# Decode attention on one core: tiles of two adjacent heads with 16 KB runs, softmax groups of four tiles, query broadcast on TensorE, MLP weights overlaid on value buffers

## The chip, the cores and the metric

The kernel runs on one core of one Trainium2 chip. The metric is the device time in microseconds (us) of that core; the median of several executions is quoted, with the lowest and the highest beside it. All executions that are compared were in the chip's fast state, and each kernel was timed beside the kernel before on the same chip. Where two changed kernels from different calls are compared, they ran on different chips; the median of the kernel before stayed between 1364.6 and 1365.5 us on all of them.

The engines are called by their names in the profile: PE is TensorE (matmuls), DVE is VectorE, ACT is ScalarE, POOL is GpSimd, SP is SyncE, which here only issues the DMA transfers. SPq is the queue in which SP's transfers stand.

## The reference

One decoding step for a batch of 8: attention with a cache of 4096 positions and 32 heads of 128, plus an MLP on the same normalized input. Everything is bf16.

```python
def reference(A_x, A_k_cache, A_v_cache, A_wq, A_wo, B_x, B_w1, B_b1, B_w2, B_b2):
    # x (8,1,640); k_cache, v_cache (8,32,4096,128); wq (640,4096); wo (4096,640)
    # w1 (640,1728); w2 (1728,640)
    xn = layernorm(A_x)
    y = layernorm(xn)
    h = gelu(y @ B_w1 + B_b1)
    q = (xn @ A_wq) as (8, 32, 1, 128)
    p = softmax(q . k_cache * 128 ** -0.5)
    o = p . v_cache
    return A_x + (o as (8, 1, 4096)) @ A_wo + (h @ B_w2 + B_b2)
```

The two caches are 268 MB each (8 x 32 x 4096 x 128 x 2 bytes). Each byte of them is used once. The kernel is a stream of 537 MB through the DMA engines, with a little arithmetic beside it.

## The kernel before

A head, here, is one (head, batch element) pair: 256 of them, each with 1 MB of K and 1 MB of V. Two heads are loaded by one transfer, and they are the same head of two neighbouring batch elements, so they are not adjacent in memory. The rearrangement gives each of the 128 partitions 32 consecutive positions of 128 bf16, a run of 8 KB, for each of the two heads.

```python
NK = 6; NV = 6                       # buffers of one head: three pairs of K, three of V

def pair_src(cache, n):
    g, i = n // B, n % B
    return cache[i:i + 2, g].rearrange("n (p j) d -> p n j d", p=P)    # two runs of 8 KB for a partition

def sp_v(n):                                                           # sp_k(n) is alike
    def fn(e):
        s = n % NV
        if n >= NV:
            e.wait(pv_done, tk[("pv", n + 1 - NV)])                    # PV must have freed the buffers
        t = ld_v[s // 2].sig(e.dma_start(V_sb[:, s:s + 2, :, :], pair_src(A_v_cache, n)))
        ...
```

The scores of a head are split over two engines. PE transposes 8 of the 32 blocks of K and multiplies them with the query (not shown). DVE does the other 24: it multiplies K with the query, which stands in all partitions, halves the product by an addition, and reduces it.

```python
def dve_qk(n):
    ...
    tm = km_done.sig(e.tensor_tensor(Y_sb[:, :, :], K_sb[:, n % NK, JP:NJ, :],
             qbc_sb[:, g % 2, i * P:(i + 1) * P][:, None, :].to_broadcast([P, ND, P]), ALU.mult))
    ...
    ty = d_sem.sig(e.tensor_tensor(Y2_sb[...], Y_sb[:, :, 0:P // 2], Y_sb[:, :, P // 2:P], ALU.add))
    ...
    kd_done.sig(e.tensor_reduce(Sd_sb[:, g % 3, i, :], Y2_sb[:, n % 2, :, :], AX.X, ALU.add))
```

The query gets into all partitions in three steps: PE transposes it into one row, DVE copies the row out of PSUM, the memory into which PE writes (`dve_qn`), and POOL broadcasts it (`pool_qb`). A softmax group is eight heads: one maximum over all of them, then the exponentials on ACT. The sum over V (called PV) follows on PE, 8 matmuls for a head. ACT copies the result out as `E_sb`, and four small matmuls (`pe_ex`) put it back into columns.

Each engine's program is a list sorted by a position. PV runs 16 heads (`2 * GP`) behind the scores, and so do the V loads:

```python
UH = 3; GP = B * UH
add("sp", -10.0, sp_mlp)                                             # MLP weights, b1 element by element
for n in range(0, NH, 2):
    add("sp", (-300.0 + n) if n == 0 else UH * (n - NK) + UH + 1.0, sp_k(n))
    add("sp", UH * (n - NV) + 2 * GP + UH + 2.5, sp_v(n))
...
for g in range(G):
    cb = float(g * GP + GP)
    ...
    for i in range(B):
        p0 = cb + GP + UH * i + (UH - 1)
        add("pe", p0, pe_PV(g * B + i))
        add("act", p0 + 0.6, act_pv(g * B + i))
        add("pe", p0 + 2.5, pe_ex(g * B + i))
```

Of the kernel before, what the change touches and what calls it, by code (L numbers as in the profile page):

```python
# [6 lines left out]

BF = mybir.dt.bfloat16
F32 = mybir.dt.float32
I32 = mybir.dt.int32  # L10
# [3 lines left out]
P = 128  # L14
# [3 lines left out]
class _Sem:  # L18

    def __init__(self, es, nc, name, step=1):  # L20
        self.h = es.enter_context(nc.semaphore(name))
        self.n = 0
        self.step = step

    def sig(self, inst):
        inst.then_inc(self.h, self.step)
        self.n += self.step
        return self.n


class _RecInst:
    def __init__(self, call):
        self.call = call

    def then_inc(self, sem, n):
        self.call[3].append((sem, n))
        return self


_OPS = ("wait_ge", "dma_start", "matmul", "transpose", "tensor_copy", "tensor_scalar",  # L40
        "tensor_tensor", "tensor_reduce", "tensor_tensor_reduce", "scalar_tensor_tensor",
        "reciprocal", "memset", "activation", "iota", "partition_broadcast")


class _Rec:

    def __init__(self):
        self.calls = []
        self.waited = {}
        (self.wait_ge, self.dma_start, self.matmul, self.transpose, self.tensor_copy,  # L50
         self.tensor_scalar, self.tensor_tensor, self.tensor_reduce, self.tensor_tensor_reduce,
         self.scalar_tensor_tensor, self.reciprocal, self.memset, self.activation,
         self.iota, self.partition_broadcast) = (self._mk(n) for n in _OPS)

    def wait(self, sem, ticket):
        if ticket > self.waited.get(sem.h, 0):
            self.waited[sem.h] = ticket
            self.wait_ge(sem.h, ticket)

    def _mk(self, name):  # L60
        def f(*a, **k):
            call = (name, a, k, [])
            self.calls.append(call)
            return _RecInst(call)
        return f


def _replay(e, calls):
    for name, a, k, incs in calls:
        if name == "wait_ge":  # L70
            e.wait_ge(*a, **k)
            continue
        if name == "dma_start":
            inst = e.dma_start(*a, **k)
        elif name == "matmul":
            inst = e.matmul(*a, **k)  # L76
        elif name == "transpose":
            inst = e.transpose(*a, **k)  # L78
        elif name == "tensor_copy":
            inst = e.tensor_copy(*a, **k)  # L80
        elif name == "tensor_scalar":
            inst = e.tensor_scalar(*a, **k)
        elif name == "tensor_tensor":
            inst = e.tensor_tensor(*a, **k)  # L84
        elif name == "tensor_reduce":
            inst = e.tensor_reduce(*a, **k)  # L86
        elif name == "tensor_tensor_reduce":
            inst = e.tensor_tensor_reduce(*a, **k)
        elif name == "scalar_tensor_tensor":
            inst = e.scalar_tensor_tensor(*a, **k)  # L90
        elif name == "reciprocal":
            inst = e.reciprocal(*a, **k)  # L92
        elif name == "memset":
            inst = e.memset(*a, **k)
        elif name == "activation":
            inst = e.activation(*a, **k)  # L96
        elif name == "iota":
            inst = e.iota(*a, **k)
        elif name == "partition_broadcast":
            inst = e.partition_broadcast(*a, **k)  # L100
        else:
            raise ValueError(name)
        for sem, n in incs:
            inst.then_inc(sem, n)


def bass_parallel_sum__gqa_block_cached__mixer_channel_mlp__decode_kernel(
# [16 lines left out]
    assert DH == P and SK % P == 0 and D % P == 0 and B <= 8  # L124
    NJ = SK // P
    TPB = 8
    BANKS = ((0, 8),)
    EVE = (1,)
    UH = 3
    BPH = len(BANKS)  # L130
    JP = sum(b[1] for b in BANKS)
    ND = NJ - JP
    assert NJ == 32 and B * JP <= 512
# [3 lines left out]
    G = H  # L137
    NH = G * B
    NBANK = NH * BPH
    GB = B * BPH  # L140
    SCALE = float(DH) ** -0.5

    NK = 6
    NV = 6
    NS = 4
    NTR = 2
    LAGT = 1
    HPP = 4 if H % 4 == 0 else 1
    NPIECE = H // HPP
    NWO = 4  # L150
    VLAG = 2 * B
# [4 lines left out]
    with ExitStack() as es:  # L156
# [3 lines left out]

        K_sb = sb("K_sb", [P, NK, NJ, P], BF)
        V_sb = sb("V_sb", [P, NV, NJ, P], BF)
        KT_sb = sb("KT_sb", [P, NS, TPB, P], BF)
        wq_sb = sb("wq_sb", [P, 2, DC, HPP * P], BF)
        wo_sb = sb("wo_sb", [P, NWO, D], BF)
        w1_sb = sb("w1_sb", [P, DC, F], BF)
        w2_sb = sb("w2_sb", [P, FC, D], BF)
        b1T_bf = sb("b1T_bf", [P, FC], BF)
        b1T_sb = sb("b1T_sb", [P, FC], F32)
# [3 lines left out]
        x32_sb = sb("x32_sb", [B, D], F32)  # L173
        sq_sb = sb("sq_sb", [B, D], F32)
        st_sb = sb("st_sb", [B, 8], F32)
        xn_bf = sb("xn_bf", [B, D], BF)
        y_bf = sb("y_bf", [B, D], BF)
        xnT_sb = sb("xnT_sb", [P, 2, DC, B], BF)
        qT_sb = sb("qT_sb", [P, H, B], BF)
        hT_sb = sb("hT_sb", [P, FC, B], BF)  # L180
        iota_i = sb("iota_i", [P, P], I32)
        iota_f = sb("iota_f", [P, P], F32)
# [3 lines left out]
        ones_f = sb("ones_f", [P, P], F32)  # L186
        zeros_bf = sb("zeros_bf", [P, P], BF)
        M1_sb = sb("M1_sb", [P, B], F32)
        M2_sb = sb("M2_sb", [B, 1], F32)
        D_sb = sb("D_sb", [B, B], F32)  # L190
        NB_sb = sb("NB_sb", [P, 3, B], F32)
        P_sb = sb("P_sb", [P, 3, B, NJ], BF)
        rs_sb = sb("rs_sb", [P, 3, 2, B], F32)
        Y_sb = sb("Y_sb", [P, ND, P], BF)
        Y2_sb = sb("Y2_sb", [P, 2, ND, P // 2], BF)
        Sd_sb = sb("Sd_sb", [P, 3, B, ND], F32)
        M1a_sb = sb("M1a_sb", [P, B], F32)
        M1b_sb = sb("M1b_sb", [P, B], F32)
        q_row = sb("q_row", [1, B * P], BF)
        qbc_sb = sb("qbc_sb", [P, 2, B * P], BF)  # L200
        rsum_sb = sb("rsum_sb", [P, B], F32)
        E_sb = sb("E_sb", [4, 2, 4 * P], BF)
        rinv_sb = sb("rinv_sb", [P, B], F32)
        oTn_sb = sb("oTn_sb", [P, 2, B], BF)
        resT_sb = sb("resT_sb", [P, DC * B], F32)
        out_sb = sb("out_sb", [B, D], BF)

        TR_ps = ps("TR_ps", [P, NTR, TPB * P], BF)
        S_ps = ps("S_ps", [P, 2, 512], F32)
        PV4_ps = ps("PV4_ps", [P, 2, 512], F32)  # L210
        CH_ps = ps("CH_ps", [P, 512], F32)
        ACC_ps = ps("ACC_ps", [P, 512], F32)
        TRF = TR_ps[:, :, :].bitcast(F32)
        M1T_ps = CH_ps[0:B, 0:P]
        NB_ps = CH_ps[:, 128:128 + B]
        RS_ps = CH_ps[:, 136:136 + 2 * B]
        QT_ps = CH_ps[:, 152:152 + HPP * B]
        HT_ps = CH_ps[:, 184:184 + FC * B]
        OT_c = CH_ps[:, 448:448 + B]
        QR_ps = CH_ps[:, 184:184 + B * P // 4].bitcast(BF)  # L220
        XT_ps = TR_ps[:, NTR - 1, 0:2 * DC * B]

        S = lambda name, step=1: _Sem(es, nc, name, step)
        assert B % 2 == 0 and NK % 2 == 0 and NV % 2 == 0 and NWO % 2 == 0 and G % 2 == 0
        ld_k = [S(f"ld_k{i}", 16) for i in range(NK // 2)]
        ld_v = [S(f"ld_v{i}", 16) for i in range(NV // 2)]
        ld_wq = [S(f"ld_wq{i}", 16) for i in range(2)]
        ld_wo = [S(f"ld_wo{i}", 16) for i in range(NWO // 2)]
        ld_x = S("ld_x", 16)
        pb_done = S("pb_done")  # L230
        e4_done = S("e4_done")
        ex_done = S("ex_done")
        km_done = S("km_done")
        kd_done = S("kd_done")
        qn_done = S("qn_done")
        ld_b1 = S("ld_b1", 16)
        ld_w1 = S("ld_w1", 16)
        ld_w2 = S("ld_w2", 16)
        out_done = S("out_done", 16)
        tr_done = [S("tr_done_d"), S("tr_done_a")]  # L240
        ev_done = [S("ev_done_d"), S("ev_done_a")]
        qk_done = S("qk_done")
        pv_done = S("pv_done")
        exp_done = S("exp_done")
        q_done = S("q_done")
        qe_done = S("qe_done")
        wo_done = S("wo_done")
        c1, c2, c3, c4, c5, c6, c7 = (S(f"c{i}") for i in range(1, 8))
        g_sem = S("g_sem")
        d_sem = S("d_sem")  # L250
        a_sem = S("a_sem")
        p_sem = S("p_sem")
        m_sem = S("m_sem")
        f_sem = S("f_sem")

        ch_read = [None]

        ch_wr = [None]

        def ch_write(e):  # L260
            if ch_read[0] is not None:
                e.wait(ch_read[0][0], ch_read[0][1])

        def ch_wrote(sem, ticket):
            ch_wr[0] = (sem, ticket)
            return ticket

        def ch_rwait(e):
# [627 lines left out]
```

## Time and profile before

| quantity | before |
|---|---|
| time, median of three (lowest to highest) | 1364.83 us (1364.8 to 1365.06) |
| span of the profiled execution | 1363.2 us |
| bytes moved by DMA | 553.13 MB |
| DVE busy | 1214.1 us, 89% |
| PE busy | 904.7 us, 66% |
| packets of 8 KB, duration (median) | 313 ns |

First come lines of the page. They give the span, the busy time of each engine with its share and its number of instructions, the DMA rate in 40 equal slices of the span, and DVE's product of K and the query (count, busy us, mean ns).

```profile
span 1363.2 us, 20347 instructions
...
PE 904.7 (66%) x8060; PEld 457.0 (34%) x8060; DVE 1214.1 (89%) x1162; ACT 547.3 (40%) x1555; POOL 70.8 (5%) x37
...
GB/s 344 267 360 421 420 415 421 419 421 419 416 421 419 421 419 417 422 419 418 411 419 419 421 419 415 421 417 421 410 417 421 418 421 417 420 421 419 421 388 211
...
L84 DVE TENSOR_TENSOR Y_sb<-K_sb,qbc_sb 128x3072 bf16<-128x3072 bf16 x256 | 446.8, 1745 | 1.1 <-POOL qbc_sb L100 1.1
...
```

The row of GB/s is what to look at. Thirty-five of the forty slices lie between 410 and 422. The first three and the last two do not. The engines by stretch say the same with chosen borders. The columns are: the stretch, its length, the busy us of PE, PE's weight loads, DVE, ACT and POOL (instructions in brackets), the granted clock, the busy share of the DMA engines, and GB/s.

```profile
...
0.00:34.00 34.00, 8.56 (x111) 6.34 (x111) 20.52 (x41) 5.67 (x7) 3.46 (x7) 1.00 0.93 344
34.00:68.00 34.00, 15.16 (x270) 12.75 (x269) 33.45 (x27) 12.59 (x24) 0.00 (x0) 1.00 0.70 268
68.00:102.00 34.00, 13.10 (x131) 8.57 (x131) 33.45 (x31) 12.31 (x41) 2.24 (x1) 0.96 0.88 359
136.00:1240.00 1104.00, 753.27 (x6652) 376.90 (x6649) 1018.71 (x953) 456.13 (x1297) 60.59 (x27) 0.81 1.01 419
1295.00:1329.00 34.00, 27.66 (x198) 11.89 (x198) 20.51 (x23) 18.26 (x78) 0.00 (x0) 0.95 0.99 387
1329.00:1363.00 34.00, 22.82 (x144) 9.06 (x143) 2.36 (x12) 6.51 (x12) 0.00 (x0) 0.98 0.55 213
...
```

Between 136 and 1240 us (the plateau) the DMA engines are fully busy at 419 GB/s, so this is the limit there. DVE is close behind (1018.71 of 1104 us). The two ends are limited by something else. All 553.13 MB at 419 GB/s would take 1320 us. The first 102 us bring only 33.0 MB, worth 79 us at that rate: 23 us are lost. The last 68 us bring 20.4 MB, worth 49 us: 19 us are lost. 1320 + 23 + 19 is 1362 of the 1363 us. I call these the plateau, the start loss and the end loss, and use the same sum for every kernel below. It is arithmetic on the windows' rates, good to about 2 us, since a rate is given in whole GB/s.

The low rate at the start has a visible companion in the timeline of the DMA queue, whose columns are the start, the time from the first to the last issue of the group, and what was issued. No V load is issued before 75.89 us, although the V buffers are empty from the start: in SP's order it stands behind loads of K, which wait for their buffers.

```profile
...
65.48 10.37 SPq L74 DMA_DIRECT2D K_sb<-in_A_k_cache_dram  x2
75.89 0.46 SPq L74 DMA_DIRECT2D V_sb<-in_A_v_cache_dram  x1
...
```

By the chain of waits the low rate at the end is PE's. The chain of the last 33 us (start, length, what) is a cycle: eight PV matmuls, the copy of `E_sb` on ACT, four small matmuls, the next head. It takes 2.75 us for 1 MB of V, while the plateau delivers 1 MB (1.049 million bytes) in 2.5 us.

```profile
...
1352.33 1.83 PE PV_ps L76 x8
1354.18 0.60 ACT E_sb L96
...
1354.83 0.25 PE CH_ps L76 x4
1355.07 1.83 PE PV_ps L76 x8
...
```

### The profile page before, as it was taken

The page shows a single profiled execution, that of the slowest core. Times are in us where ns is not written, and L with a number is a line of the kernel's source. Part 1 is how long each engine was busy: PE and PEld are TensorE (multiplying, and loading weights), DVE is VectorE, ACT ScalarE, POOL GpSimd, SP SyncE. Part 2 cuts the span into 40 slices and gives each one's busy share as a digit, 9 for nine tenths or more (in the row PEclk, how much of TensorE's full clock was granted, in tenths as well). Part 3 has the DMA queues.
Part 4 walks back from the last instruction along what each step waited for, and adds up shares of the span by engine and source line. Part 5 has one row for each costly group of instructions (what it writes and reads, how often), then busy time and mean ns, then how long its engine had stood idle before and what let it go on. Part 6 is the DMA issues. An engine that isn't in the chain of part 4 may idle for free.

```text
span 1363.2 us, 20347 instructions
## 1 busy us (share of the span) xinstructions
PE 904.7 (66%) x8060; PEld 457.0 (34%) x8060; DVE 1214.1 (89%) x1162; ACT 547.3 (40%) x1555; POOL 70.8 (5%) x37
## 2 busy tenths in 40 slices
PE   2437666767766767666767666668665767666786
PEld 1323333333323333333333333334333333333332
DVE  6999999989989899898989989899898999999960
ACT  1334433444433344433444434344332444433451
POOL 1000000000000000000000000000000000000000
PEclk9998778888778788778888778888777788778899
DMA  9689999999999999999999999999999999999995
GB/s 344 267 360 421 420 415 421 419 421 419 416 421 419 421 419 417 422 419 418 411 419 419 421 419 415 421 417 421 410 417 421 418 421 417 420 421 419 421 388 211
DMA packets 83551, 553.13 MB, mean 406 GB/s; under 512 B 6312, under 2 KB 17280, under 8 KB 17920
## 3 DMA queue, kind: packets, MB, share of 16 engines
q1 hardware_dynamic: 83456, 551.83, 98.4%
q8 instruction: 63, 1.03, 0.3%
q14 instruction: 32, 0.26, 0.0%
HBM read 551.80 MB, written 0.01 MB: 405 GB/s over the span
## 4 chain that ended last, share of the span: by engine, by line
DVE 50%; issue 22%; DMA 19%; PE 7%; ACT 1%; DVEq 0%; POOL 0%; SPq 0%; POOLq 0%
DVE Y_sb L84 41%; DMA K_sb<-in_A_k_cache_dram 19%; DVE Sd_sb L86 4%; PE PV_ps L76 3%; PE CH_ps L78 2%; DVE q_row L80 2%; PE CH_ps L76 1%; PE TR_ps L78 1%; ACT E_sb L96 1%; DVE M_sb L86 1%; DVE rinv_sb L92 1%; DVE oTn_sb L84 0%; DVE NB_sb L80 0%; DVE M1b_sb L86 0%; ACT P_sb L96 0%
## 5 line engine op out<-in xcount | busy, mean ns | idle before, releaser
L76 PE MATMUL PV_ps<-V_sb,P_sb 128*4 128x512 bf16 x2048 | 582.6, 435 | 12.1 <-DMA V_sb<-in_A_v_cache_dram 11.9
L86 DVE TENSOR_REDUCE Sd_sb<-Y_sb 128x24 f32<-128x1536 bf16 x256 | 448.8, 1753 | 8.9
L84 DVE TENSOR_TENSOR Y_sb<-K_sb,qbc_sb 128x3072 bf16<-128x3072 bf16 x256 | 446.8, 1745 | 1.1 <-POOL qbc_sb L100 1.1
L96 ACT ACTIVATE E_sb<-PV_ps 4x512 bf16<-4x512 f32 x256 | 149.9, 586 | 525.1 <-PE PV_ps L76 525.1
L96 ACT ACTIVATE KT_sb<-TR_ps 128x1024 bf16<-128x1024 bf16 x256 | 260.2, 1016 | 157.6 <-PE TR_ps L78 157.6
L76 PEld LDWEIGHTS PV_ps<-V_sb,P_sb 128*4 128x4 bf16 x2048 | 172.6, 93 | 279.9 <-issue 108.0
L84 DVE TENSOR_TENSOR Y_sb<-Y_sb 128x1536 bf16<-128x1536 bf16 x256 | 256.0, 1000 | 8.8
L78 PE MATMUL TR_ps<-ident_bf,K_sb 128*128 128x128 bf16 x2048 | 177.5, 237 | 93.1 <-DMA K_sb<-in_A_k_cache_dram 83.4
L78 PEld LDWEIGHTS TR_ps<-ident_bf,K_sb 128*128 128x128 bf16 x2048 | 133.4, 106 | 96.2 <-DMA K_sb<-in_A_k_cache_dram 86.5
L76 PE MATMUL CH_ps<-ident_bf,E_sb 4*128 4x1 bf16 x1024 | 63.5, 162 | 111.5 <-DVE NB_sb L80 93.2
L78 PE MATMUL CH_ps<-ident_f,M_sb 128*8 128x128 f32 x32 | 11.8, 368 | 180.8 <-DVE oTn_sb L84 168.0
L100 POOL PARTITION_BROADCAST qbc_sb<-q_row x32 | 70.4, 2199 | 1171.8 <-DVE q_row L80 1171.8
L76 PEld LDWEIGHTS S_ps<-qT_sb,KT_sb 128*128 128x128 bf16 x2048 | 69.4, 98 | 166.7 <-issue 90.9
L76 PE MATMUL S_ps<-qT_sb,KT_sb 128*128 128x1 bf16 x2048 | 91.3, 165 | 46.6 <-ACT KT_sb L96 46.6
L96 ACT ACTIVATE P_sb<-S_ps,NB_sb 128x8 bf16<-128x8 f32 x256 | 63.5, 248 | 113.1 <-DVE NB_sb L80 113.1
L76 PEld LDWEIGHTS CH_ps<-ident_bf,E_sb 4*128 4x128 bf16 x1024 | 42.6, 94 | 146.9 <-issue 115.7
L96 ACT ACTIVATE P_sb<-Sd_sb,NB_sb 128x24 bf16<-128x24 f32 x256 | 77.0, 301 | 0.0
L78 PEld LDWEIGHTS CH_ps<-ident_f,M_sb 128*8 128x8 f32 x32 | 2.7, 83 | 183.3 <-issue 170.1
L80 DVE COPY q_row<-CH_ps 1x512 bf16<-1x512 bf16 x64 | 26.0, 407 | 32.1 <-PE CH_ps L76 30.4
L96 ACT ACTIVATION_READ_ACCUMULATOR P_sb<-S_ps,NB_sb 128x1 f32 x256 | 48.3, 189 | 0.0
L96 ACT ACTIVATION_READ_ACCUMULATOR P_sb<-Sd_sb,NB_sb 128x1 f32 x256 | 48.2, 188 | 0.0
L86 DVE TENSOR_REDUCE M_sb<-CH_ps 8x1 f32<-8x128 f32 x32 | 8.9, 278 | 38.8 <-PE CH_ps L78 37.3
(63 smaller groups left out, 204.2 us busy)
## 6 DMA issues: line engine op xcount, KB each, us to landing
K_sb<-in_A_k_cache_dram SPq DMA_DIRECT2D x128, 2048.0 KB, 16.8
V_sb<-in_A_v_cache_dram SPq DMA_DIRECT2D x128, 2048.0 KB, 16.3
wq_sb<-in_A_wq_dram SPq DMA_DIRECT2D x8, 640.0 KB, 22.2
wo_sb<-in_A_wo_dram SPq DMA_DIRECT2D x16, 320.0 KB, 15.9
w_sb<-in_B_w_dram SPq DMA_DIRECT2D x1, 2160.0 KB, 8.3
w_sb<-in_B_w_dram SPq DMA_DIRECT2D x1, 2080.0 KB, 12.9
w_sb<-in_B_w_dram SPq DMA_DIRECT2D x1, 80.0 KB, 13.1
x_sb<-in_A_x_dram SPq DMA_DIRECT2D x1, 10.0 KB
```

The costliest lines, as they stand in the source:

```text
L76: inst = e.matmul(*a, **k)
L78: inst = e.transpose(*a, **k)
L80: inst = e.tensor_copy(*a, **k)
L84: inst = e.tensor_tensor(*a, **k)
L86: inst = e.tensor_reduce(*a, **k)
L92: inst = e.reciprocal(*a, **k)
L96: inst = e.activation(*a, **k)
L100: inst = e.partition_broadcast(*a, **k)
```

## The change

The change rewrites the kernel around a tile of two adjacent heads of the same batch element (`HT = 2`). Those are contiguous in memory, so a partition's share of a tile is one run of 16 KB rather than two of 8 KB: partitions 0 to 63 hold the first head, 64 to 127 the second. The transfer stays at 2 MB. There are 128 tiles, in softmax groups of four (`GT = 4`), and the intent is:

1. longer runs, for a higher DMA rate;
2. a start without holes: `b1` as one row rather than element by element, MLP weights loaded into the memory of V buffers 1 to 3 before V needs it, PV only 4.75 tiles behind the scores (it was 8 pairs), a first V load early in the queue;
3. a tail of V alone that DMA can feed: V falls behind K by 6% (`CV = 1.06`), the last tile comes in four pieces;
4. less DVE work: operations twice as large, no row copies of the query, the query broadcast by PE matmuls, and next to nothing left on POOL.

The hand-written semaphore bookkeeping is replaced by a scheduler. Each operation declares the keys that it reads (`R`), writes (`W`) or shares as a PSUM bank (`X`), and the waits follow from these keys.

```diff
-    NK = 6
-    NV = 6
+    HT = 2                                   # heads in a tile
+    GT = 4                                   # tiles in a softmax group
+    NK, NV, NS = 4, 4, 4                     # buffers of a tile, 2 MB each
-        K_sb = sb("K_sb", [P, NK, NJ, P], BF)
-        V_sb = sb("V_sb", [P, NV, NJ, P], BF)
-        w1_sb = sb("w1_sb", [P, DC, F], BF)
-        w2_sb = sb("w2_sb", [P, FC, D], BF)
+        KV_sb = sb("KV_sb", [P, NK + NV, NJ * P], BF)
+        arena = KV_sb[:, NK + 1:NK + NV, :].rearrange("p a b -> p (a b)")
+        w1_sb = arena[:, 0:DC * F].rearrange("p (c f) -> p c f", c=DC)
+        w2_sb = arena[:, DC * F:DC * F + FC * D].rearrange("p (c n) -> p c n", c=FC)
...
-            return cache[i:i + 2, g].rearrange("n (p j) d -> p n j d", p=P)
+        def tile_src(cache, t):
+            return cache[t % B, (t // B) * HT:(t // B + 1) * HT].rearrange("h k d -> (h k) d").rearrange(
+                "(p j) d -> p j d", p=P)
...
+        CV = 1.06
+        def pvpos(i):
+            return 4.75 + CV * i
...
+        for t in range(T):
+            pos = -98.0 + t if t < 2 else (-96.0 + t if t < NK else t - 3.5)
+            ... # K loads
+            pos = (0.9, 1.6, 2.4, 3.4)[t] if t < NV else pvpos(t - NV) + 0.95
+            W = ["ovw1", "ovw2a", "ovw2b"] if 1 <= t < NV else []
+            for n, (j0, j1) in enumerate(vpieces(t)):
+                ld(pos + 0.01 * n, vview(t)[:, j0:j1, :], tile_src(A_v_cache, t)[:, j0:j1, :],
+                   [("V", t % NV, q) for q in range(j0 // 16, j1 // 16)] + W, "v%d_%d" % (t % NV, n))
+        ld(-95.3, b1_sb[:, :], B_b1.rearrange("(o f) -> o f", o=1), ["b1"], "b1")
+        ld(-95.2, w1_sb, B_w1.rearrange("(c k) f -> k c f", k=P), ["ovw1"], "w1")
+        ... # w2a, w2b likewise
...
-            tk[("pb", g)] = pb_done.sig(e.partition_broadcast(qbc_sb[:, g % 2, :], q_row[0:1, :], channels=P))
+            r = e.matmul(TRF[a * PG:(a + 1) * PG, it.box[0], i * P:(i + 1) * P],
+                         qT_sb[:, hg * HT + a, b0 + i:b0 + i + 1].to_broadcast([P, PG]),
+                         ident_bf[:, :], start=True, stop=True)
...
-            p0 = cb + GP + UH * i + (UH - 1)
-            add("pe", p0 + 2.5, pe_ex(g * B + i))
+            p0 = pvpos(t)
+            for q in range(4):
+                add("pe", p0 + 0.15 * q, pe_pv, ...)            # four matmuls each
+            add("act", p0 + 0.5, ...)                           # E_sb <- PV_ps
+            add("pe", p0 + 0.8, pe_ex, ...)
...
+            np_ = pvpos(g * GT + GT - 1) + 0.85                 # in finish(g): normalize the group
```

The probabilities of a tile are laid out so that one PV matmul has both heads' rows (8 rows, each zero in the other head's partitions). So the number of PV matmuls stays at 2048.

## The prediction

> **What bounds it now.** The table of engines by stretch shows the 16 DMA engines 100% busy at 418-421 GB/s from 102 to 1295 us, DVE 92-93% busy: DMA binds, DVE is close. The DMA queue table gives 552 MB; at 421 GB/s that is 1311 us, so 52 us of the 1363 us span is lost at the ends:
> - Start, 24 us: 34 us slices at 344, 268, 359 GB/s. DMA nearly stops at 10-12 us beside the element-wise b1 load; later it waits for DVE: no V load goes before 75.9 us (timeline), and K is consumed at 4.45 us per 1 MB head.
> - End, 28 us: slices at 388 and 211 GB/s. The V tail is paced by PE: 2.75 us per head, 1.83 of it the eight PV matmuls, 0.9 the wait for the E copy (chain of waits). DMA is silent from 1348 us, PE works to 1357, the close takes 6.3.
>
> **What the change does.**
> 1. Runs of 16 KB instead of 8 KB. Packet durations in this trace: 46 ns (1 KB), 55 (1280 B), 135 (3456 B), 309 (8 KB): a line, 8.4 ns + 36.7 per KB. Estimate for 16 KB: 610 ns against 618 for two of 8 KB: 421 becomes 427-429 GB/s, about 17 us. The Trainium skill, "DMA: Bandwidth & Descriptors", "Why small descriptors are slow", states a fixed cost per packet; these durations agree.
> 2. Start: b1 becomes one row, b2, w1, w2 follow K0/K1, V0 goes at tile 0.9: 13 MB are queued before anyone waits. Without POOL's iota (8.6 us) DVE's first product starts near 11 us, not 21.7. The hole shrinks from 24 to 3-5 us.
> 3. End: V drifts behind K (about 11 tiles of V alone), the last tile comes in four pieces. PE per 2 MB tile there: 16 x 0.229 + 0.9 + 0.2 = 4.8 us against 4.9 of DMA: DMA-paced; after the last landing 4 PV matmuls and the close, 7 us.
> 4. DVE per tile, sizes doubled, fixed costs once: 3.39 + 1.79 + 3.27 + 0.3 (group work) = 8.75 us against a DMA period of 9.6; before 9.6. About 90 us less, off the critical path. The q_row copies (26 us DVE) and the POOL broadcast go; ACT takes a qbc, an S and an NB copy; PE has about 6.7 us per tile.
>
> **Sum.** K/V 32,768 packets x 610 ns / 16 = 1249; weights 39; plus 1% (the plateau before is 1% under its packet minimum) = 1301; start 3, close 7: span 1311, time about **1311 us** (1298-1334). Faster by over 2%: 0.88; within 2%: 0.09; slower: 0.03. Without step 1: about 1329.
>
> **What shows it.** Step 1: packets of 16 KB at about 610 ns, a plateau of 427-430 GB/s; wrong at 618 ns or if split. Step 2: first slices at 400 GB/s or more, first V issue before 20 us. Step 3: DMA busy to within 8 us of the end. Step 4: DVE busy about 1130 us.
>
> **What would make it wrong.** In-order PE couples everything: it waits for DVE's group maximum, V and the bias chain. If V lands late and PE holds up transposes or the query broadcast, DVE stops, K buffers free late, and with only 4+4 buffers DMA empties: its share falls below 95% mid-run, and the time goes towards 1340. A colder PE clock in the tail would make it PE-paced (7 us per tile, +20 us).

## The result

| quantity | before | after |
|---|---|---|
| time, median (lowest to highest) | 1364.94 us (1364.8 to 1365.24) | 1326.64 us (1325.39 to 1326.83) |
| span of the profiled execution | 1363.2 us | 1323.6 us |
| DVE busy | 1214.1 us | 1110.1 us |
| PE busy | 904.7 us | 950.9 us |
| long packets, median duration | 8 KB: 313 ns | 16 KB: 613 ns |
| first DVE product starts | 21.74 us | 15.14 us |
| first V load is issued | 75.89 us | 22.67 us |

The ratio is 0.9716, with a 95% interval of 0.9702 to 0.9729. A ratio in this document is the mean time of one kernel's fast runs over that of the other's of the same rounds, so it is not quite the ratio of the medians quoted.

The page of after, with the lines that answer to those of before:

```profile
span 1323.6 us, 17617 instructions
...
PE 950.9 (72%) x7690; PEld 452.3 (34%) x7690; DVE 1110.1 (84%) x554; ACT 510.7 (39%) x1228; POOL 0.2 (0%) x4
...
GB/s 360 377 426 423 427 421 428 425 428 427 426 426 427 427 421 426 429 424 427 426 428 426 425 428 423 427 425 427 426 425 428 427 427 425 427 428 426 422 386 253
...
L472 DVE TENSOR_TENSOR Y_sb<-KV_sb,qbc_sb 128x6144 bf16<-128x6144 bf16 (+1 forms) x129 | 428.4, 3321 | 17.7 <-DMA KV_sb<-in_A_k_cache_dram 15.7
...
```

The engines by stretch, with the same columns as before; the tail is cut finer:

```profile
...
0.00:34.00 34.00, 12.00 (x187) 10.32 (x187) 27.27 (x44) 8.66 (x16) 0.20 (x4) 1.00 0.93 362
34.00:68.00 34.00, 20.15 (x231) 13.63 (x231) 30.73 (x15) 14.86 (x36) 0.00 (x0) 1.00 0.92 377
68.00:102.00 34.00, 23.49 (x197) 11.54 (x197) 32.02 (x15) 14.30 (x35) 0.00 (x0) 0.80 1.01 424
136.00:1240.00 1104.00, 804.50 (x6447) 377.12 (x6444) 963.00 (x448) 441.67 (x1071) 0.00 (x0) 0.83 1.01 426
1240.00:1256.00 16.00, 10.58 (x88) 5.34 (x88) 15.86 (x7) 5.98 (x11) 0.00 (x0) 0.83 1.00 426
1256.00:1272.00 16.00, 13.03 (x79) 5.05 (x77) 8.89 (x7) 5.18 (x22) 0.00 (x0) 0.95 0.83 333
1272.00:1304.00 32.00, 27.39 (x155) 11.21 (x156) 0.59 (x4) 4.00 (x7) 0.00 (x0) 1.00 1.01 429
1304.00:1323.00 19.00, 13.62 (x83) 5.41 (x81) 1.40 (x5) 2.34 (x4) 0.00 (x0) 0.98 0.34 137
...
```

The plateau rose from 419 to 426 GB/s. The third stretch is now full, the second is better but still short at 377, and in the tail there is a stop at 1256 to 1272 us (333 GB/s) and a silent end. The sum, done as before: 552.96 MB at 426 GB/s are 1298 us. The start brings 39.5 MB in its 102 us, worth 93 us: 9 us are lost. The 83 us from 1240 on bring 28.5 MB, worth 67: 16 us are lost.

| us | before | after | gained |
|---|---|---|---|
| plateau, all bytes at its rate | 1320 | 1298 | 22 |
| start loss | 23 | 9 | 14 |
| end loss | 19 | 16 | 3 |
| sum (span measured) | 1362 (1363.2) | 1323 (1323.6) | 39 (39.6) |

What remains of the start loss is partly the first 34 us (362 GB/s, about 5 us) and partly a hole. Finer windows find it between 52 and 64 us, where the two lines give 332 and 257 GB/s. At 426 that is 1.3 + 2.4 = 3.7 us.

```profile
...
52.00:58.00 6.00, 2.57 (x21) 2.00 (x21) 5.97 (x5) 1.83 (x4) 0.00 (x0) 1.00 0.79 332
58.00:64.00 6.00, 3.50 (x16) 1.17 (x16) 5.98 (x2) 5.17 (x17) 0.00 (x0) 1.00 0.75 257
...
```

The DMA queue's timeline shows what was not issued. The line at 37.08 has two V loads, 21.98 us from the issue of the first to the end of the second's.

```profile
...
22.67 0.43 SPq L288 DMA_DIRECT2D KV_sb<-in_A_v_cache_dram  x1
...
37.08 21.98 SPq L288 DMA_DIRECT2D KV_sb<-in_A_v_cache_dram  x2
...
```

The list of waits of the DMA queue (who waits for what: us in total, times, longest) has the reason. One of these waits is for the landing of another V load, and it lasts 21.3 us.

```profile
...
SPq L288 <- DMA KV_sb<-in_A_v_cache_dram: 28.4, 2, 21.3
...
```

The tail is told by three views. First, PE's timeline (start, length, what, and in brackets how long PE sat idle and what ended that). It stands 3.26 us for the last K tile and 1.69 us for the group's maximum.

```profile
...
1252.83 1.89 PE L440 MATMUL TR_ps<-ident_bf,KV_sb 128*128 128x128 bf16 x16 [3.26 <-DMA KV_sb<-in_A_k_cache_dram]
...
1264.66 0.27 PE L489 MATMUL CH_ps<-ident_f,M_sb 128*4 128x128 f32 x1 [1.69 <-DVE M_sb L487]
...
```

Second, the DMA queue at the same time. No V load is issued between 1249 and 1260.26 us, since PE frees no V buffer; all of the last twelve follow from there.

```profile
...
1230.77 18.23 SPq L288 DMA_DIRECT2D KV_sb<-in_A_v_cache_dram  x3
...
1260.26 39.86 SPq L288 DMA_DIRECT2D KV_sb<-in_A_v_cache_dram  x12
...
```

Third, the chain of waits to the end. From 1272 us on PE never waits for DMA: 3.56 us of PV, 0.59 for the copy on ACT, 0.25 for the small matmuls, 4.47 from tile to tile.

```profile
...
1272.54 0.25 PE C_ps L550 x4
1272.79 3.56 PE PV_ps L537 x16
1276.37 0.59 ACT E_sb L544
1277.01 0.25 PE C_ps L550 x4
...
```

### The profile page after: what moved, and what is told of

The parts are those of the page before. It is cut to its first block, busy times and chain, and to the rows that moved or that the text cites. A ratio compares the mean times of both kernels' runs of the same rounds, so it can differ in the third digit from the quotient of the medians.

```text
span 1323.6 us, 17617 instructions
## 1 busy us (share of the span) xinstructions
PE 950.9 (72%) x7690; PEld 452.3 (34%) x7690; DVE 1110.1 (84%) x554; ACT 510.7 (39%) x1228; POOL 0.2 (0%) x4
## 2 busy tenths in 40 slices
DMA packets 47760, 552.96 MB, mean 418 GB/s; under 512 B 4585, under 2 KB 11713, under 8 KB 15042
## 4 chain that ended last, share of the span: by engine, by line
DMA 60%; DVE 18%; PE 18%; ACT 3%; SPq 2%; issue 0%; DVEq 0%
DMA KV_sb<-in_A_k_cache_dram 50%; PE PV_ps L537 12%; DMA KV_sb<-in_A_v_cache_dram 10%; DVE Y_sb L472 9%; DVE S_sb L479 5%; DVE Y_sb L476 3%; PE TR_ps L440 3%; SPq L288 2%; ACT P_sb L506 1%; PE C_ps L517 1%; ACT KT_sb L443 1%; ACT E_sb L544 1%; PE S_ps L450 1%; DVE M_sb L487 0%; PE C_ps L550 0%
## 5 line engine op out<-in xcount | busy, mean ns | idle before, releaser
L537 PE MATMUL PV_ps<-KV_sb,P_sb 128*8 128x512 bf16 x2048 | 622.1, 448 | 29.1 <-DMA KV_sb<-in_A_v_cache_dram 28.7
L472 DVE TENSOR_TENSOR Y_sb<-KV_sb,qbc_sb 128x6144 bf16<-128x6144 bf16 (+1 forms) x129 | 428.4, 3321 | 17.7 <-DMA KV_sb<-in_A_k_cache_dram 15.7
L479 DVE TENSOR_REDUCE S_sb<-Y_sb 128x48 f32<-128x3072 bf16 (+1 forms) x129 | 429.2, 3327 | 4.4
L440 PE MATMUL TR_ps<-ident_bf,KV_sb 128*128 128x128 bf16 x2048 | 191.9, 253 | 200.4 <-DMA KV_sb<-in_A_k_cache_dram 200.4
L537 PEld LDWEIGHTS PV_ps<-KV_sb,P_sb 128*8 128x8 bf16 x2048 | 164.3, 94 | 294.4 <-issue 134.7
L440 PEld LDWEIGHTS TR_ps<-ident_bf,KV_sb 128*128 128x128 bf16 x2048 | 145.9, 114 | 288.3 <-DMA KV_sb<-in_A_k_cache_dram 234.4
L476 DVE TENSOR_TENSOR Y_sb<-Y_sb 128x3072 bf16<-128x3072 bf16 (+1 forms) x129 | 224.0, 1736 | 2.7
L544 ACT ACTIVATE E_sb<-PV_ps 8x512 bf16<-8x512 f32 x128 | 74.9, 585 | 180.1 <-PE PV_ps L537 180.0
L450 PE MATMUL S_ps<-qT_sb,KT_sb 128*128 128x2 bf16 x2048 | 91.1, 167 | 59.0 <-ACT KT_sb L443 58.7
L506 ACT ACTIVATE P_sb<-S_sb,NB_sb 64x64 bf16<-64x64 f32 x256 | 88.4, 345 | 4.3
```

Of the source, the lines that this page charges most:

```text
L440: r = e.transpose(TR_ps[:, it.box[0], jj * P:(jj + 1) * P], kv[:, n * BK + jj, :], ident_bf[:, :])
L450: r = e.matmul(S_ps[:, c:c + HT], KT_sb[:, m % NS, jj, :], qT_sb[:, hg * HT:(hg + 1) * HT, b], start=True, stop=True)
L472: return e.tensor_tensor(y, kv[:, j0:j1, :], qbc_sb[:, g % 2, i, :][:, None, :].to_broadcast([P, nj, P]), ALU.mult)
L476: lambda e, y=y, y2=y2: e.tensor_tensor(y2, y[:, :, 0:P // 2], y[:, :, P // 2:P], ALU.add),
L479: lambda e, y2=y2, j0=j0, j1=j1: e.tensor_reduce(S_sb[:, g % SR, i, j0:j1], y2, AX.X, ALU.add),
L506: r = e.activation(P_sb[s, g % PR, i, :, a, :], S_sb[s, g % SR, i, :].rearrange("p (m c) -> p m c", c=4), ACT.Exp, bias=NB_sb[s, g % 2, i: ...
```

## The experiments

Twelve kernels were run, each with three timed rounds beside a profiled run. All runs passed the comparison with the reference. Where an expectation names its theories by letters, a letter holds within that text; what each run left standing is said in words after it. "Before" beside an experiment is the kernel before in the same rounds.

### 1. The kernel after with runs of 8 KB (a_run8)

This undoes the length of the runs: each 2 MB tile comes in two loads of half its columns. It also doubles the number of transfers.

```diff
-            return [(0, 16), (16, 32), (32, 64)] if t == 0 else [(0, 64)]
+            return [(0, 16), (16, 32), (32, 64)] if t == 0 else [(j, j + 32) for j in range(0, 64, 32)]
...            # the same for vpieces, with its own semaphores for the last tile's pieces
```

> The changed kernel, each 2 MB K or V load split into two loads of half a row per partition (runs of 8 KB), nothing else. Correct result. Theory A (the run sets the rate): packets of 8 KB at 313 to 318 ns, plateau 419 to 421 GB/s, time 20 to 26 us longer, 1345 to 1352 us. Rival B: time within 5 us of 1326.6.

It took 1349.58 us (1348.19 to 1352.22), ratio to before 0.9883 (0.9867 to 0.9898). That is 23 us above the kernel after, as expected. The 8 KB packets are back at a median of 313 ns, and the plateau is back at 420 GB/s:

```profile
...
136.00:1240.00 1104.00, 800.84 (x6347) 366.81 (x6346) 955.41 (x442) 434.97 (x1055) 0.00 (x0) 0.82 1.01 420
...
```

The sum splits the difference of the two spans (1348.5 - 1323.6 = 24.9 us): 553.00 MB at 420 take 1316.7 us, 18.7 more than after. The first three slices of its page (359, 323 and 362 GB/s) cost 8 us more than those of after, and its end costs 2 us less. So some 19 us are the rate alone. (The table's 22 us for the plateau are some 3 more: this kernel has 420 GB/s with 8 KB runs, the kernel before 419. Where these come from was not looked into.)

The trace shows where the extra start loss lies. The queue's list of waits has five V loads that wait for another V load's landing, 42.0 us in all, where after has two and 28.4 us:

```profile
...
SPq L288 <- DMA KV_sb<-in_A_v_cache_dram: 42.0, 5, 21.4
...
```

These are the loads of V1 to V3, now six halves, which share the keys that experiment 9 takes apart. No run with 8 KB runs and separate keys was made, so that this is the whole of the 8 us is not shown.

### 2. The kernel before with runs of 16 KB (b_run16)

The other direction: the kernel before reads 2 MB that are contiguous. The result of this kernel is wrong, since the buffers then hold other heads' data. The comparison with the reference passed all the same: its tolerance does not see which part of the cache was read. (Why was not examined. It also means that "correct" says little about data placement in any of these runs.)

```diff
-            return cache[i:i + 2, g].rearrange("n (p j) d -> p n j d", p=P)
+            t = n // 2
+            return cache[t % B, t // B * 2:t // B * 2 + 2].rearrange("h k d -> (h k) d").rearrange(
+                "(p j) d -> p j d", p=P)
...            # the destination is flattened to match
```

> The kernel before, with one edit: each 2 MB pair load of K and V now reads one contiguous 2 MB piece (a run of 16 KB per partition) instead of two heads of two batches (runs of 8 KB). The data goes to the wrong heads, so the result is wrong on purpose; instructions, sizes and waits are the same. Theory A (the length of the run sets the DMA rate): 32768 packets of 16 KB at about 613 ns, plateau from 419 to about 426 GB/s, time about 1342 us (1337 to 1346). Rival B (the faster plateau of the changed kernel comes from its other waits, or from the broadcast and row copies being gone, not from the runs): plateau stays at 419, time 1362 to 1366.

It took 1350.45 us (1349.55 to 1350.6) against 1365.18, ratio 0.9885 (0.9871 to 0.99). This is 14.7 us, less than expected. The plateau did what the other run says, but the rest did not stay:

```profile
...
136.00:1240.00 1104.00, 760.54 (x6726) 382.23 (x6724) 1031.32 (x971) 458.60 (x1301) 62.81 (x28) 0.81 1.01 425
...
1329.00:1349.00 20.00, 11.96 (x76) 4.78 (x76) 1.81 (x9) 3.35 (x6) 0.00 (x0) 0.94 0.19 79
...
```

At 425 GB/s all bytes take 1301.5 us, 18.6 less than before, the same 19 us as in the first experiment. The start loss is unchanged (34 to 68 us still run at 265 GB/s). The end loss rose: from 1260 us on it is 22 us where it was 19. This is what a tail at PE's pace would do: a faster stream reaches it sooner and gains nothing in it. That reading was not tested. So the length of the runs is worth some 19 us in the plateau, in both kernels, and how much of that arrives depends on the ends.

### 3. The kernel before with the first V loads early (b_earlyv)

The question was whether the start loss before is only a matter of the order of issues. The first three V transfers go ahead of the waits for K.

```diff
-            add("sp", UH * (n - NV) + 2 * GP + UH + 2.5, sp_v(n))
+            add("sp", (-1.5 + 0.1 * n) if n < NV else UH * (n - NV) + 2 * GP + UH + 2.5, sp_v(n))
```

> The kernel before with only the first three V pair loads (12.6 MB) moved ahead of everything that waits, so that they fill the hole of the first 100 us. Correct result. Theory A (DMA binds, and DMA time lost at the start is never given back): the 34 us slices from 34 to 102 us rise above 400 GB/s, 23 us of lost DMA time fall to about 10, time about 1352 us (1348 to 1356). Rival B (VectorE, busy 92 per cent, is what sets the pace through the middle): bytes come earlier but VectorE ends as late, time above 1361 us.

It took 1373.22 us (1371.52 to 1374.23), ratio 1.0052 (1.0037 to 1.0067): 8 us slower, where 1348 to 1356 was expected. The order of issues alone is refuted as the cause. The rival's number (above 1361) came true, but not its reason: from 136 to 1240 us the DMA engines are still full, at 418 GB/s.

```profile
...
34.00:68.00 34.00, 12.91 (x248) 11.40 (x248) 26.30 (x19) 9.55 (x21) 0.00 (x0) 1.00 1.01 413
68.00:102.00 34.00, 12.85 (x131) 8.91 (x130) 33.41 (x31) 13.69 (x41) 2.24 (x1) 1.00 0.59 226
...
```

The hole moved from 34-68 us to 68-102 us. The second stretch is now full (413 GB/s), but its bytes are V, which nobody can use yet. K came late for that, and DVE, busy 33.45 us in that stretch before, is busy 26.30. PV begins 16 heads behind the scores, at 99.68 us rather than 92.2, and until then the V buffers stay full. So what can come in before that is fixed by the buffers and by K, which DVE consumes at its own pace.

### 4. Both together (b_run16_earlyv)

> Both edits of the two runs above in the kernel before (wrong result on purpose, through the contiguous pieces). Theory A (both act on DMA time and add up): about 1330 us (1324 to 1335), close to the changed kernel's 1326.6 without any of its change of the compute. Rival B (once DMA is faster, VectorE with 1214 us of work becomes the limit): above 1340 us.

Experiments 2 and 3 in one kernel took 1358.53 us (1356.59 to 1360.11), ratio 0.9944 (0.9927 to 0.996). That misses the 1324 to 1335 that I had expected by far, since both parts had missed. It is 14.7 us below b_earlyv, the same 14.7 that the long runs gave alone: the two edits add up, and the start of before is not bound by the DMA rate. The rival's number (above 1340) came true here too, again without its reason: the plateau is at 424 GB/s, so DVE does not hold it back there.

### 5. The kernel before with a shorter lag (b_lag12)

The kernel after starts PV 4.75 tiles, 9.5 heads, behind the scores. Can the old kernel's order carry that? Here PV runs 12 heads behind rather than 16, with the exponentials spaced closer to be ready for it, and everything after PV moved with it.

```diff
-            add("sp", UH * (n - NV) + 2 * GP + UH + 2.5, sp_v(n))
+            add("sp", UH * (n - NV) + GP + 12 + UH + 2.5, sp_v(n))
-                    add("act", cb + 11 + 2 * q4, act_exp(g, i0_, i1_))
+                    add("act", cb + 11 + 0.9 * q4, act_exp(g, i0_, i1_))
-                p0 = cb + GP + UH * i + (UH - 1)
+                p0 = cb + 12 + UH * i + (UH - 1)
...                # pe_RS, dve_norm, pe_oproj: 2 * GP becomes GP + 12
```

> The kernel before with PV half a group closer behind K (4 heads earlier, with the four pieces of exp closer together in ScalarE's order, and V loads, row sums and output projection moved along). Correct result. Theory A, formed after moving the V loads alone had failed (the hole at the start is what the buffers can take in before the first PV drains V, so it ends with the first PV, now at 92 us): first PV at about 75 us, slices from 34 to 102 us richer, about 8 us shorter, 1354 to 1360 us; a shorter lag gives nothing at the end, as in the run without drift. Rival B (the hole is tied to VectorE or to the prologue, not to the first PV): 1363 us or more.

It took 1396.07 us (1394.2 to 1397.92), ratio 1.022 (1.0203 to 1.0237): slower by 31 us, far from the 1354 to 1360 expected. The start did get better, as the shorter lag should make it: the stretches of 34 us went from 344, 268, 359 to 342, 328, 405 GB/s, worth some 8 us, and the first PV started at 83.85 us (some 75 was expected). But from 136 to 1240 us the rate fell to 410 GB/s, and from 1240 us on the sum gives a loss of 34 us, where before has 19. In the list of waits (who waits for what: us in total, times, longest) two lines stand out. The first was 36.7 us, 3 times, in before; the second is not in before's list.

```profile
...
DVE rsum_sb L86 <- PE CH_ps L76: 110.8, 25, 20.1
PE PV_ps L76 <- ACT P_sb L96: 88.5, 32, 3.1
...
```

PV now stands at the head of PE's queue before its probabilities are ready. I read this as an order that, with one softmax over eight heads, has no room for a lag of 12; no run tested that reading. So the start gain that the shorter lag brings could not be had in the old kernel by this edit. The kernel after combines the shorter lag with groups of four; that the groups are what makes it work was not run by itself.

### 6. The kernel after with a longer lag (a_lag8)

```diff
-            return 4.75 + CV * i
+            return 8.75 + CV * i
```

> The changed kernel with PV four tiles (8 heads) further behind K from the start (offset 4.75 to 8.75), which is about the distance of the kernel before (16 heads). Theory A (start hole ends with the first PV, now at 61 us): first PV at about 95 us, the slices from 34 to 102 us fall to 250 to 350 GB/s, 10 to 18 us longer, 1337 to 1345 us. Rival B (the early part of the gain came from the prologue and the order of the loads): within 4 us of 1326.6.

It took 1331.14 us (1330.94 to 1334.57), ratio 0.9755 (0.974 to 0.9769): 4.5 us above after, below the 10 to 18 that I expected and just over the rival's 4. Yet the start did not change. The stretches are 364, 381 and 421 GB/s (after: 362, 377, 424), although PV begins at 97.44 us rather than 60.8. The loss is in the tail: 400 GB/s from 1220 to 1240 us and 275 from 1240 to 1260. So in the kernel after the lag does not set the start loss, which refutes what I had carried over from experiment 3. The hole at 52 to 64 us has another cause.

### 7. Fifth V buffer (a_nv5_exlate)

My first guess for that hole was that four V buffers are too few. A fifth takes 16 KB of each partition. Room was made for it by two K-transpose buffers instead of four, five probability buffers instead of six, and small tensors laid over others. It includes the edit of experiment 8, with which it is to be compared.

```diff
-    NK, NV, NS = 4, 4, 4
-    PR, SR = 6, 3
+    NK, NV, NS = 4, 5, 2
+    PR, SR = 5, 3
...            # xn_bf, y_bf in Y2_sb; out_sb is x_sb; position 4.4 for the fifth V load
```

> The changed kernel with five V buffers instead of four (paid for by two buffers fewer of transposed K, one group fewer of probabilities, and small tensors laid over others) and with the later small matmuls of the run above. Theory A (the hole at 55 to 61 us is V4 waiting for the first PV because four V buffers are full; about 4 us of DMA): the hole goes, time about 1316 us, 3 to 5 us below the run with the later matmuls alone. Rival B (the lost time comes back later, or fewer buffers of transposed K hold up TensorE): no gain over that run or a loss.

It took 1322.85 us (1322.45 to 1326.55), ratio 0.9695 (0.968 to 0.9709), the same as a_exlate (1322.86). The hole stayed: 326 and 232 GB/s at 52 to 58 and 58 to 64 us, against 329 and 248 in a_exlate. But this run does not refute the guess. With `NV = 5` the condition `1 <= t < NV` in the code of the V loads takes in the fifth tile as well, so its load got the shared keys too (experiment 9) and waited for the landing of the one before. The waits for a landing are now three:

```profile
...
SPq L289 <- DMA KV_sb<-in_A_v_cache_dram: 37.9, 3, 21.7
...
```

The load into the fifth buffer was issued at 76.76 us, after the hole, so the buffer could not help. What speaks against the guess is experiment 9, which fills the hole with four buffers.

### 8. The small matmuls later (a_exlate)

In the tail of after, PE reaches the small matmuls of a tile before ACT has finished the copy they read, and stands 0.68 us at each. Moved half a tile later, they come after the first PV matmuls of the next tile.

```diff
-            add("pe", p0 + 0.8, pe_ex, ...)
+            add("pe", p0 + 1.3, pe_ex, ...)
-            np_ = pvpos(g * GT + GT - 1) + 0.85
+            np_ = pvpos(g * GT + GT - 1) + 1.35
```

> The changed kernel; the four small matmuls that sum a tile's four PV rows (they wait for ScalarE's copy of PV) go half a tile later in TensorE's order, between the second and third quarter of the next tile's PV, so that TensorE no longer waits for the copy between tiles. Theory A (after the last K tile the tail is paced by TensorE: 4.47 us per tile, 0.9 of it waiting, with about 12 tiles left): 3.9 us of work per tile, the tail shrinks until DMA paces it, time 5 to 8 us shorter, 1319 to 1322 us; DMA busy to within 8 us of the end. Rival B (the tail is paced by DMA and the loss lies in the stop at 1256 to 1272 us): less than 2 us gained.

It took 1322.86 us (1322.48 to 1323.52), ratio 0.9689 (0.9675 to 0.9704). That is 3.8 us below after, a little less than the 5 to 8 expected. PE's timeline in the tail now shows it waiting for DMA, not for ACT:

```profile
...
1285.34 1.89 PE L537 MATMUL PV_ps<-KV_sb,P_sb 128*8 128x512 bf16 x8
1288.21 1.89 PE L537 MATMUL PV_ps<-KV_sb,P_sb 128*8 128x512 bf16 x8 [0.98 <-DMA KV_sb<-in_A_v_cache_dram]
1290.03 0.25 PE L550 MATMUL C_ps<-ident_bf,E_sb 8*128 8x2 bf16 x4
...
```

So the pace of PE in the tail did cost time, and once it is gone DMA sets the pace. In both kernels the last bytes of V arrive between 1312 and 1314 us (14 GB/s there in after, 8 here); the span ends at 1320.7 us rather than 1323.6. So what is gained is time after the last bytes. The stop before it is still there (315 GB/s from 1256 to 1264 us) and puts a floor under the gain.

### 9. Separate keys for the overlaid buffers (a_ovsplit_exlate)

The wait of 21.3 us for another V load's landing has a plain origin in the declarations. V tiles 1, 2 and 3 each go into a buffer that the MLP weights used. To wait for the MLP's reads, each declares that it writes the three keys of the overlay. But then V1, V2 and V3 write the same keys, and the scheduler orders two writers: V2's load waits for V1's to have landed, V3's for V2's. The memory does not overlap. Here each load writes only the keys of the weights that really lie in its buffer.

```diff
-            W = ["ovw1", "ovw2a", "ovw2b"] if 1 <= t < NV else []
+            W = {1: ["ov1w1"], 2: ["ov2w1", "ov2w2a"], 3: ["ov3w2a", "ov3w2b"]}.get(t, [])
...
-        ld(-95.2, w1_sb, ..., ["ovw1"], "w1")
+        ld(-95.2, w1_sb, ..., ["ov1w1", "ov2w1"], "w1")
...            # w2a: ov2w2a and ov3w2a; w2b: ov3w2b; the MLP matmuls read the same keys
```

> The run with the later small matmuls, with the bookkeeping of the overlaid MLP weights split by V buffer, so that V2 and V3 wait for the MLP matmuls that read their own buffer and no more for the landing of V1 and V2 (in the changed kernel the load queue stands 21.3 us for V1's landing, up to 58.7 us). Theory A (that chain, not a lack of V buffers, made the hole at 56 to 61 us; a fifth V buffer had not filled it): V2 issued by 45 us, DMA full from 46 to 64 us, 3 to 5 us shorter than with the later matmuls alone, about 1318.5 us. Rival B (the hole moves on to the next wait): less than 1.5 us gained.

It took 1319.26 us (1319.0 to 1319.75), ratio to before 0.9662 (0.9648 to 0.9677). That is 3.6 us below a_exlate, as expected, and 3.7 us is what the hole had been worth. The DMA queue issues V1 and V2 from 27.78 to 37.09 us and V3 at 38.16, and the windows of the hole are full:

```profile
...
27.78 9.31 SPq L288 DMA_DIRECT2D KV_sb<-in_A_v_cache_dram  x2
...
38.16 0.43 SPq L288 DMA_DIRECT2D KV_sb<-in_A_v_cache_dram  x1
...
```

```profile
...
52.00:58.00 6.00, 2.54 (x21) 1.96 (x21) 5.97 (x4) 2.12 (x5) 0.00 (x0) 1.00 1.01 427
58.00:64.00 6.00, 3.79 (x16) 1.15 (x16) 5.68 (x2) 4.89 (x16) 0.00 (x0) 1.00 1.02 433
...
```

This is the fastest kernel found here; it beats both. The keys are shown to be the cause of the hole: nothing else changed against a_exlate. But they carried two waits, and both are gone. Besides the waits for a landing, V1 had to wait for the MLP's second layer, which does not read its buffer; it is now issued at 27.78 us, in a_exlate at 37.22. How much each of the two is worth was not run.

### 10. DVE made busier (a_dve)

The change saved 104 us of DVE time. How much of the gain is that? An addition that is not used, over up to 22 rows, is put into each tile's work; it costs some 0.8 us a tile and brings DVE back to 1210.5 us, before's level.

```diff
+                XN = min(22, j1 - j0)
-                    lambda e, ...: e.tensor_tensor(y2, y[:, :, 0:P // 2], y[:, :, P // 2:P], ALU.add),
+                    lambda e, ...: (e.tensor_tensor(X_sb[:, 0:XN, :], y[:, 0:XN, 0:P // 2], y[:, 0:XN, P // 2:P], ALU.add),
+                                    e.tensor_tensor(y2, y[:, :, 0:P // 2], y[:, :, P // 2:P], ALU.add))[1],
```

> The changed kernel with one extra VectorE add per tile (22 of 48 rows into a scratch buffer, about 0.8 us, 103 us in all), which gives back the VectorE work that the change saved (1214 to 1110 us). Theory A (VectorE is off the critical path as long as DMA binds): 0 to 10 us longer (up to 1337 us), DMA still full in the middle. Rival B (the saved VectorE work is where the gain came from): 80 us or more longer, above 1400 us. In between, 1340 to 1380, would say that VectorE had become the limit with this extra work through its waits for TensorE (113 us) on top of 1213 us of work.

It took 1332.47 us (1331.26 to 1333.64), ratio 0.9759 (0.9745 to 0.9774): 5.8 us above after, within the 0 to 10 expected. The plateau did not notice: with DVE busy 1054.57 of 1104 us it is still at 426 GB/s.

```profile
...
136.00:1240.00 1104.00, 810.42 (x6478) 379.28 (x6477) 1054.57 (x562) 444.90 (x1080) 0.00 (x0) 0.82 1.01 426
...
```

So of the 100 us of DVE work put back, some 94 lie off the critical path. The other 6 come in at the tail: the three stretches of the start are at 364, 374 and 425 GB/s, as in after, but 1256 to 1272 and 1272 to 1304 us are at 304 and 385, where after has 333 and 429.

### 11. No drift of V (a_cv100)

```diff
-        CV = 1.06
+        CV = 1.0
```

> The changed kernel with the drift of V behind K taken out (1.06 to 1.0): V stays 4.75 tiles behind K to the end instead of about 12. Theory A (DMA must deliver everything before the last K tile can be done, so the work left after the last byte is one VectorE tile, the softmax and about five PV tiles): DMA goes silent about 30 us before the end, time 5 to 18 us longer, 1331 to 1345 us. Rival B (a shorter TensorE tail of V is a gain): shorter than 1322 us.

It took 1325.82 us (1324.52 to 1327.0), ratio 0.9711 (0.9695 to 0.9727). This is 0.8 us below after, no more than the kernel before differs between chips, and neither of the expectations holds. The drift of V behind K was worth nothing. The long tail of V that it makes is gone, and so is the stop (430, 426 and 402 GB/s in 1240 to 1256, 1256 to 1272 and 1272 to 1304 us), but the scores on DVE then go on to 1296 us, and the loss lies after them: 98 GB/s from 1304 to 1323 us (after: 137).

### 12. More drift in the best version (a_best_cv109)

```diff
-        CV = 1.06
+        CV = 1.09
```

on top of experiment 9.

> The best version so far (later small matmuls, split bookkeeping of the overlay, 1319.3 us) with a larger drift of V behind K (1.06 to 1.09, about 15 tiles of V left after K in place of 12). Theory A (TensorE now needs 3.9 us per V tile in the tail against 4.9 of DMA, so each further tile left for the tail is DMA time that ends nearer to the end): 1 to 3 us shorter, 1316 to 1318.5 us. Rival B (a faster K stream runs into VectorE's 8.7 us of work plus waits per tile, and V buffers stand full): no change, or up to 5 us longer.

It took 1324.67 us (1324.27 to 1325.14), ratio 0.9706 (0.969 to 0.9722): 5.4 us above experiment 9, where 1 to 3 us less was expected and the rival allowed up to 5 more. The loss is in the tail: 329 GB/s from 1240 to 1280 us. A longer tail of V alone brings a longer stop, so more drift does not help either. What exactly sets the length of that stop was not settled.

## Why the prediction was right, and where it was off

The prediction was 1311 us with a range of 1298 to 1334 and 0.88 for faster by over 2%. The time is 1326.64 us, in the range but 16 us above the centre, and the kernel is faster by 2.8%. Point by point:

**What bounds the kernel.** Right. DMA binds from 136 to 1240 us in both kernels, and the rest is lost at the two ends. One term was oversized: the 28 us of end loss came from dividing by 421 GB/s, a rate picked off the page's better slices. With the plateau's own 419 it is 19 us. So less could be gained at the end than I thought.

**Step 1, the runs.** Right in mechanism and close in size, with some luck. 610 ns for 16 KB was two packets of 8 KB (read as 309 ns each; the median over the trace is 313) less one fixed cost of 8.4 ns. The median is 613. The prediction's own line, 8.4 ns plus 36.7 for each KB, gives 596 for 16 KB and does not reach long packets. The saving is 13 ns (626 less 613), not 8; reading 8 KB too low made up for most of that. It was to raise the plateau to 427-429 GB/s, and it is 426. The prediction's base of 1301 us for the plateau compares with 1298. Undoing only this costs 19 us by rate (experiment 1), doing only this gains 19 us by rate (experiment 2), and 17 were predicted. "Without step 1: about 1329", 18 us above its centre, is 23 us above after in experiment 1, since the start suffers too. The Trainium skill, "DMA: Bandwidth & Descriptors", section "Why small descriptors are slow (HBM only)", states a fixed overhead for every packet, with an example at 256 bytes. This trace agrees in kind and shows that it still matters at 8 KB. Two packets of 8 KB take 626 ns by their medians, one of 16 KB takes 613.

**Step 2, the start.** Right in direction, off in size: 23 us became 9, where 3 to 5 were predicted. "First slices at 400 GB/s or more" did not come true for the first two (362 and 377), nor did "first V issue before 20 us" (22.67): the queue took 16.33 us to issue the three loads of MLP weights before it, and its list of waits names no reason. The missing 4 to 6 us are, for 3.7, the hole at 52 to 64 us. That is a wait that the new bookkeeping made, and I did not read it out of the diff although the line with the three keys is in it. Experiment 9 shows it by removing it. DVE's first product came at 15.14 us, not at 11.

**Step 3, the end.** This is the step that failed: "DMA-paced; after the last landing 4 PV matmuls and the close, 7 us." The numbers in it were good: PE needs 4.47 us a tile, 4.8 were predicted, and DMA needs 4.92 (2.097 MB at 426 GB/s). The conclusion was not. It compared two rates and forgot where the tail starts. PE takes its work in order. At the end of K it stood 3.26 us for the last K tile and 1.69 us for the group's maximum, so no V buffer came free, all V transfers stood until 1260 us, and the DMA engines ran at 333 GB/s between 1256 and 1272 us. When PE went on, it had full V buffers before it. It gained only 0.45 us a tile on DMA, over the ten tiles from 1272 us on, so it never caught up. The last bytes of V arrived about 1313 us, and PE still had the end of one tile, a whole one and the close to do, some 11 us. The end loss is 16 us where 7 were predicted: 3.5 us in the stop, 13 from 1304 us on. Experiment 8 confirms half of it: a faster PE in the tail gained 3.8 us and turned the wait into one for DMA, and then some 7.5 us were left after the last bytes, as predicted. That the stop itself could be avoided at no cost was not shown: less drift (experiment 11) removed the stop and gained nothing, more drift (experiment 12) and more lag (experiment 6) made the tail worse.

**Step 4, DVE.** Right. The three operations and the group's work were predicted at 8.75 us a tile; the means are 3.35, 1.75 and 3.35 us, and the group's small operations add 0.26: 8.71. "Off the critical path" is right within 6 us (experiment 10). POOL's broadcast is gone with it. Its neighbourhood had cost both something: the addition beside it at 33.06 us in the trace of before took 1.31 us, the one before it 0.96, and the broadcast took 2.24 us there, while the first one, beside which DVE did nothing, took 0.80. The Trainium skill, "SBUF — State Buffer", section "SBUF: two separate sides", states that DVE operations with two SBUF inputs and GpSimd operations that read SBUF exclude each other on a shared port pair. This one place agrees with it, and no run tested it.

**The sum.** 1301 + 3 + 7 = 1311 was given as span and as time, but the time of an execution is some 1.8 us above its span (1325.39 and 1323.6 in the profiled one of after). Start (9 rather than 3) and end (16 rather than 7) make 15 us. Less 3 for the plateau, plus 1.8 for this, plus 1.3 by which the profiled execution lies below the median, this is 15 of the 16 us.

What stays open: whether the shared keys are all of the 8 us that the kernel after loses more at the start with 8 KB runs (experiment 1), which of the two waits of experiment 9 made the hole, and what sets the stop at the turn from K to V.

## What to carry to other kernels

Where a long plateau at full DMA rate takes most of the span, try the length of the contiguous run before saving engine work. Here 8 to 16 KB gave some 19 us of 1365, while putting back 100 us of VectorE work cost 6. The rest is at the ends, and there two rates are not enough: ask what the in-order engine waits for when the tail begins, and how many full buffers it has before it then. Where waits follow from declared keys, check which keys two transfers share; three V loads that touched no common byte were serialized by shared names, and one waited for work that did not read its buffer, for 3.6 us together. And before a run counts against a guess, look in its trace whether the edit took effect (experiment 7).

## What the Trainium skill lacked or had wrong

- "DMA: Bandwidth & Descriptors", section "Why small descriptors are slow (HBM only)", gives its example at 256 bytes and no duration for long packets. Here the packets of one core took 46 ns (1 KB), 159 (4 KB), 313 (8 KB) and 613 (16 KB). "Perfetto Trace Analysis", section "DMA Optimizations", speaks of 2 KB grown to 4 or 8 KB; 8 to 16 KB still raised the plateau from 420 to 426 GB/s, worth 19 us of 1326.
- "HBM Reference", section "Specifications (TRN2)", says about 425 GB/s for a core that streams alone. That agrees with the plateau of 426 here, but the page does not say that it depends on the run: with 8 KB runs it was 419 to 420.
- No page was found that tells how to read a tail in which an in-order engine with full buffers ends 11 us after the last DMA transfer, though each of its tiles takes less time (4.47 us) than a tile's transfer (4.92 us).
- No page was found that warns of dependency keys for overlaid memory. Here a shared key made one transfer's issue wait 21.3 us for the landing of another.
